# Chunk-selected attention with a capacity-limited expert layer: gating the last head pair from its exponents, and the second expert product in rounds of four 32-column tiles

## Chip, cores and metric

The kernel runs on one core of one Trainium2 chip, in one launch. The metric is the device time of that launch in microseconds (us), as the median of several runs. The engines are PE (matrix multiplication, with PEld for its weight loads), DVE (vector), ACT (scalar, activation functions), POOL (general purpose; it also starts the indirect transfers) and SP (starts most other transfers).

## The reference, cut to what matters

```python
# attention: 4 batches, 8 heads, 768 tokens, 64 wide; keys in chunks of 32
ub = sum over d of max(q * k_min(chunk), q * k_max(chunk))      # causal chunks only
sel = the 6 chunks with the highest ub of each query
scores = where(sel & causal, q @ k.T / 8, -1e9)
attn = softmax(scores);  out = attn @ v
x = out.transpose(0, 2, 1, 3).reshape(3072, 512)                # a row per token
# experts: 8, capacity 80 tokens each
logits = x @ w_gate;  e = argmax(logits);  gate_w = softmax(logits)[e]
for e in range(8):
    tok = the 80 tokens of expert e with the highest gate_w
    h = relu(x[tok] @ w1[e])                                    # 512 -> 1024
    out[tok] = gate_w[tok] * (h @ w2[e])                        # 1024 -> 512
# every other row of the output is zero
```

## The kernel before, in words

**Attention, 16 head pairs.** The loop `for i in range(NP)` (NP is 16) takes two heads of one batch at a time; four pairs make a batch. For each pair PE computes upper bounds (`bounds`, L473), DVE turns them into a table of chunks that are not selected (`bounds_out`, L480 to L492), and PE turns that table over (`unselT`, L498). `scores` then runs six steps, each a product of keys and queries (L510) plus a mask product (L525) into one of two accumulators SC, and ACT takes the exponents into the tile EXB (L530). POOL cuts the causal diagonal out of each exponent tile (L540) and adds the tiles up into ES (L549). `values` multiplies the exponents by V (L560) into OB, and ACT copies the result to oT (L564). The values are not yet divided by the sum of their exponents.

**A pair is finished in the next pair's iteration.** `sums` multiplies oT by the gate weights (L569), which gives the pair's share of the logits, and ES by ones (L583), which gives the sums of the exponents. `sums_out` turns both over on DVE (L574 to L577) and `scale_lg` divides (L614). `rows` transposes oT to token rows (L604), `scale_rows` divides these into the tile xp (DVE L624), and SP stores xp in `x_rows` in DRAM (L626). There is one xp tile: the next write to it waits until the store before has landed.

**Gate and capacity, per batch.** After a batch's fourth pair DVE adds the logits, takes the maximum and the argmax, and ACT the exponent (`gate_in`, `gate_exp`, `gate`: L633 to L647); gt6 holds the winning probability of each token. The 80 best tokens of each expert come from counting, for each token, how many of its expert's tokens are better: `rank_row` spreads gt6 along a row (PE L670, ACT L672), `rank_pred` makes a second row a hair smaller (ACT L675), `rank_cmp` and `rank_diag` compare (DVE), `rank_count` adds the comparisons on PE (L727), `rank_slot` and `rank_hot` turn the counts to slots (DVE L732 to L741), `table` collects slots on PE (L750) and `merge` puts them into the running list of 80 a expert (DVE L746 to L770). The running list is itself kept sorted (`sort_rows`, `sort_rank`, `sort_apply`). For the first three batches this work is spread over the next batch's iterations; the last batch's stands alone behind the loop, with forms of its own (`last_cmp` L712 to L715, `last_diag` L703) and with dummy products `keep_warm` (L814) on PE.

**The last pair.** In iteration 15 the values follow the scores. Behind the loop `sums_last` (L595) adds the exponents from their tiles and then runs `sums_lg` (L569) on oT; so the last batch's gate begins with the last pair's values.

**Experts.** `merge` ends with `idx`, 80 row numbers for each expert. POOL starts a `gather` of these rows from `x_rows` for each expert (L958). `turn` transposes a gathered tile (PE L967, ACT L970), `up` is the product with w1 (PE L978: 32 products of 80 columns) with ACT (L985) and DVE (L987) taking the positive part into hT, and `down` the product with w2: eight accumulated products with hT as the stationary side, 80 columns wide, and 512 columns of w2 moving (L1009). The last expert's is cut into two halves (L994). DVE multiplies by the gate weight gT (L1013, L997), and POOL scatters the 80 rows to the output (L1015). The order on PE is turn(e+1), up(e), down(e-1).

**Order and waits.** All instructions are written in one order by hand; each engine runs its own in that order. The helper `op` derives the waits from named resources that an operation reads and writes. Weights are loaded by POOL (`wload`, L411 and L414): w2 of expert 6 and w1 of expert 7 at the end of iteration 14, w2 of expert 7 into the first part of EXB behind the loop.

## Time and profile before

| what | value |
|---|---|
| median of 3 runs (lowest to highest) | 299.59 us (299.08 to 306.82) |
| the profiled execution | 297.99 us |
| its span, first to last instruction | 296.2 us |
| mean granted PE clock | 0.975 |
| PE busy | 277.8 us (94%) |
| DVE busy | 208.8 us (70%) |
| POOL busy | 233.8 us (79%) |
| ACT busy | 145.0 us (49%) |
| start of the last pair's scores on PE | 231.13 us |
| end of the last pair's values on PE | 245.25 us |
| gt6 of the last batch ready | 250.05 us |
| first gather on POOL | 260.22 us |
| first turn on PE | 262.90 us |
| last product on PE | 290.65 us |

The span is 1.8 us shorter than the execution it belongs to, and that execution is 1.6 us below the median. Times in the text are microseconds from the start of the span. In a list of instructions in order of time a row gives start, duration, engine, line, operation, output and inputs, and in brackets the idle time ahead of it with what ended it; an "x8" means that eight neighbours of one kind are merged. In the chain of waits a row is one stretch of the path that ended last: start, length, and the engine and line that it was spent on.

### The profile page before, as it was taken

To read this page: it belongs to the slowest core of one execution; us is meant where nothing else is said; L and a number is where in the kernel's file an instruction comes from. 1 tells how busy PE (TensorE), PEld (TensorE's weight loads), DVE (VectorE), ACT (ScalarE), POOL (GpSimd) and SP (SyncE) were. 2 spreads that over 40 slices of the span, in tenths; PEclk is the share of its full clock that TensorE was granted. 3 is DMA by queue.
4 is the path that set the end of the run, shared out by engine and by line. 5 is a ranking of instruction groups with operands and counts; after the bars stand their busy time and mean duration, and the time that the engine had idled before them with its cause. 6 is when DMAs were issued, how large, how long until landed. Compare 5 with 4: busy or idle time off the path is not lost.

```text
span 296.2 us, 8268 instructions
## 1 busy us (share of the span) xinstructions
PE 277.8 (94%) x3400; PEld 171.9 (58%) x3402; DVE 208.8 (70%) x561; ACT 145.0 (49%) x197; POOL 233.8 (79%) x299
## 2 busy tenths in 40 slices
PE   7679999999999999999999999999999999579992
PEld 7245565655656565656565657565646566247662
DVE  3867282746797989659889898898897886803332
ACT  2155646565657555545764546566654541512210
POOL 5049999989898999989899999898999993055332
PEclk9779999999999999999999999999999999879999
DMA  9998999998999999999999999899438299511212
GB/s 150 172 156 135 294 190 138 291 229 154 165 159 197 183 164 186 182 187 169 165 186 177 168 174 214 133 192 361 169 69 158 21 175 191 99 41 47 61 45 66
DMA packets 155141, 47.52 MB, mean 160 GB/s; under 512 B 139128, under 2 KB 147444, under 8 KB 155104
## 3 DMA queue, kind: packets, MB, share of 16 engines
q1 hardware_dynamic: 138528, 27.95, 47.9%
q0 software_dynamic: 13440, 18.67, 38.7%
q10 hardware_dynamic: 3136, 0.39, 0.9%
q8 instruction: 26, 0.43, 0.6%
q14 instruction: 11, 0.09, 0.1%
HBM read 53.10 MB, written 10.75 MB: 216 GB/s over the span
## 4 chain that ended last, share of the span: by engine, by line
PE 67%; POOL 16%; DVE 6%; DMA 6%; issue 2%; ACTq 1%; POOLq 0%; ACT 0%; DVEq 0%
PE SC L510 21%; PE OB L560 18%; POOL ES L549 12%; PE SC L525 4%; PE OB L1009 4%; DMA x_rows<-xp 4%; PE SC L978 4%; PE M L583 4%; PE OB L604 3%; POOL EXB L540 3%; PE M L473 2%; PE M L569 2%; PE MB L498 2%; DMA kn<-in_k_dram 1%; DMA qn<-x_rows,idx 1%
## 5 line engine op out<-in xcount | busy, mean ns | idle before, releaser
L530 ACT ACTIVATE EXB<-SC 128x1024 f32<-128x1024 f32 x96 | 86.2, 916 | 49.2 <-PE SC L525 47.9
L549 POOL TENSOR_TENSOR ES<-ES,EXB 128x256 f32<-128x256 f32 (+1 forms) x108 | 105.7, 991 | 4.9
L510 PE MATMUL SC<-qT,kT 64*128 64x512 f32 (+3 forms) x512 | 99.5, 479 | 1.0 <-ACT EXB L530 1.0
L560 PE MATMUL OB<-EXB,vn 128*64 128x256 f32 (+2 forms) x704 | 72.3, 360 | 0.4 <-POOL EXB L540 0.4
L560 PEld LDWEIGHTS OB<-EXB,vn 128*64 128x64 f32 x704 | 47.0, 137 | 23.6 <-issue 9.0
L510 PEld LDWEIGHTS SC<-qT,kT 64*128 64x128 f32 x512 | 42.6, 191 | 25.0 <-issue 15.1
L549 POOL TENSOR_TENSOR ES<-EXB 128x768 f32<-128x768 f32 (+1 forms) x32 | 49.9, 1558 | 2.7
L525 PE MATMUL SC<-unsT,ind 64*128 64x128 bf16 (+5 forms) x256 | 38.3, 294 | 0.8 <-ACT unsT L500 0.8
L564 ACT ACTIVATE oT<-OB 128x512 f32<-128x512 f32 (+1 forms) x32 | 15.6, 489 | 44.3 <-PE OB L560 44.3
L540 POOL TENSOR_SCALAR_AFFINE_SELECT EXB<-EXB 128x256 f32<-128x256 f32 x80 | 35.1, 448 | 0.0
L525 PEld LDWEIGHTS SC<-unsT,ind 64*128 64x128 bf16 x256 | 13.0, 96 | 18.3 <-issue 8.0
L574 DVE STREAM_TRANSPOSE M<-M 128x192 f32<-128x192 f32 x16 | 6.3, 394 | 23.1 <-PE M L583 21.2
L441 DVE STREAM_TRANSPOSE qT<-qn 128x768 f32<-128x768 f32 x16 | 15.6, 972 | 9.4 <-PE SC L525 9.4
L624 DVE TENSOR_TENSOR xp<-OB,rden 128x768 bf16<-128x768 f32 x16 | 15.3, 955 | 7.0 <-PE OB L604 6.1
L445 ACT ACTIVATE rq<-qT 128x768 f32<-128x768 f32 x16 | 13.5, 843 | 9.7 <-DVE qT L441 8.9
L451 DVE STREAM_TRANSPOSE kT<-kn 128x768 f32<-128x768 f32 x16 | 15.5, 967 | 3.6 <-DMA kn<-in_k_dram 3.5
L1015 POOL DMA_INDIRECT out_dram<-EXB,idx x7 | 6.5, 931 | 12.8 <-DVE EXB L1013 7.8
L958 POOL DMA_INDIRECT qn<-x_rows,idx x4 | 3.9, 982 | 15.7 <-DVE gT L770 13.2
L455 DVE TENSOR_REDUCE kmm<-kT 128x24 f32<-128x768 f32 x16 | 15.2, 950 | 0.5
L457 POOL TENSOR_TENSOR kmm<-kmx,kmm 128x24 f32<-128x24 f32 x16 | 7.3, 454 | 10.4 <-DVE wg L833 6.8
L456 DVE TENSOR_REDUCE kmx<-kT 128x24 f32<-128x768 f32 x16 | 15.1, 943 | 0.0
L487 DVE MAX8 top<-M 128x8 f32<-128x8 f32 (+4 forms) x160 | 14.6, 166 | 0.6
(163 smaller groups left out, 404.7 us busy)
## 6 DMA issues: line engine op xcount, KB each, us to landing
w1s<-in_moe_w_dram POOLq DMA_DIRECT2D x8, 1024.0 KB, 9.2
w2s<-in_moe_w_dram POOLq DMA_DIRECT2D x7, 1024.0 KB, 10.6
qn<-in_q_dram SPq DMA_DIRECT2D x64, 96.0 KB, 3.3
vn<-in_v_dram SPq DMA_DIRECT2D x32, 192.0 KB, 3.5
out_dram<-w1s SPq DMA_DIRECT2D x4, 1536.0 KB, 9.1
kn<-in_k_dram SPq DMA_DIRECT2D x60, 96.0 KB, 3.2
x_rows<-xp SPq DMA_DIRECT2D x16, 192.0 KB, 4.7
EXB<-in_moe_w_dram POOLq DMA_DIRECT2D x1, 1024.0 KB, 10.8
```

The source lines that it names most:

```text
L441: op("dve", lambda: ve.transpose(qT[j][:], qn[s][:].rearrange("p a b c -> p (a b c)")), r=[f"qn{s}{g}" for g in range(4)], w=[f"qT{j}"])
L451: op("dve", lambda: ve.transpose(kT[j][:], kn[s][:].rearrange("p a b c -> p (a b c)")), r=[f"kn{s}{g}" for g in range(4)], w=[f"kT{j}"])
L455: op("dve", lambda: ve.tensor_reduce(kmm[j][:, 0, 0:NCH], kv, AX, ALU.min), r=[f"kT{j}"], w=[f"kmm{j}"])
L456: op("dve", lambda: ve.tensor_reduce(kmx[:], kv, AX, ALU.max), r=[f"kT{j}"], w=["kmx"])
L510: op("pe", lambda: pe.matmul(o, kT[j][pr, ts(kt)], qT[j][pr, q0:q1], start=True, stop=False), r=[f"kT{j}", f"qT{j}"], w=[f"SC{s}"], inc=False)
L525: op("pe", lambda: pe.matmul(o, ind[pr, ts(kt)], unsT[j][pr, b0 - 128:q1 - 128], start=False, stop=True), r=[f"ind{h}", f"unsT{j}"], w=[f" ...
L530: op("act", lambda: ac.activation(Ex(st, None, 0, W), src, ACTF.Exp, scale=SCALE), r=[f"SC{s}"], w=[f"E{st}"])
L540: op("gp", lambda: gp.affine_select(ad, a, pattern=[[0, 2], [1, 128]], compare_op=ALU.is_ge, fill=0.0, base=0, channel_multiplier=-1), r=[ ...
L549: op("gp", lambda: gp.tensor_tensor(o, in0, in1, ALU.add), r=[f"E{s2}", f"E{first[0]}"] if first else [f"E{s2}"] + kt, w=kt)
L560: op("pe", lambda: pe.matmul(OB[pr, q0:q1], vn[s][:, kt, h, :], ex, start=(n == 0), stop=last), r=[f"vn{s}{h}", "ES0" if st is None else f ...
L564: op("act", lambda: ac.activation(oT[:, q0:q1], OB[:, q0:q1], ACTF.Copy), r=[f"O{bk}"], w=[f"oT{bk}"])
L624: op("dve", lambda: ve.tensor_tensor(xo, xi, rx, ALU.mult), r=["O0", "O1", "rden"], w=["xp"])
```

## The change

1. **Last pair's logits from the exponents.** V of the last pair is loaded a second time, in the layout of keys (`load_vk`, four transfers on SP in iteration 12), turned over on DVE (`vw_turn`) and multiplied by the gate weights on PE (`vw_mm`). The result VW has for each key the head's share of 8 logits, and ones in the columns for the sums. The new `sums_last` multiplies the exponent tiles by VW, and gives logits and sums together. It needs neither oT nor ES: POOL leaves out the additions of the last pair and only cuts the diagonals.
2. **Values behind the gate.** The last pair's `values` move behind `sums_last`; the gate, the row of gt6 and a part of the comparisons are written among them. `rows` and `scale_rows` of the last pair come later, in the middle of the comparisons.
3. **Comparisons without the second row.** `rank_pred` is gone for the last batch: `last_low` (less than) and `last_high` (at most) compare with the one row, which is copied in two halves by ACT and DVE (`last_row`). Each token tile needs a lower part, the diagonal and an upper part. The dummy products stand between the counts (`last_count`).
4. **Work of the batch before.** `rank_hot`, the digits and the columns of batch 2 move ahead of `bounds_out` in iteration 14 (`rank_late`), its `table` and `merge` from iteration 15 to the end of 14; `sort_rows` and `sort_rank` move forward in iteration 15; both halves of `clear_xg` stand in iteration 14.
5. **Second expert product in rounds.** Each expert's 80 columns of hT are padded to 96, three blocks of 32. A round takes four blocks, each as the stationary side of a product of its own on 32 columns of PE, each with its own expert's w2 moving. Four experts make three rounds; six rounds replace eight `down`s. `spread` brings gate weights and row numbers to the 128 rows of each round (PE, DVE). A scatter has 128 rows, and there are six.

```diff
+                def vw_turn():
+                    op("dve", lambda: ve.transpose(kT[0][:], kn[0][:].rearrange("p a b c -> p (a b c)")),
...
+                    op("dve", lambda: ve.memset(VW, 0.0), w=["qT0"])
...
+                def vw_mm():
+                    p = (NP - 1) % NPB
+                    for kt in range(NT):
+                        op("pe", lambda: pe.matmul(MBf[:, kt * 16:kt * 16 + 16], kT[0][:, ts(kt)], wg[:, p, 0:16], start=True, stop=True),
...
+                def sums_last():
+                    pieces = [(0, 0, 0, 0, 512), (0, 3, 0, 512, S), (1, 1, 0, 128, 640), (2, 2, 0, 256, S), (4, 3, 256, 512, S),
+                              (3, 4, 0, 384, S), (1, 4, 384, 640, S), (5, 5, 0, 640, S)]
+                    for n, (kt, st, c0, q0, q1) in enumerate(pieces):
                         for h in range(2):
+                            a = Ex(st, h, c0, q1 - q0).rearrange("p (t c i) -> p t c i", c=4, i=32)
                             for c in range(4):
+                                op("pe", lambda: pe.matmul(M0[c * 32:c * 32 + 32, q0 // 4:q1 // 4], VW[:, h, kt, :], a[:, :, c, :],
...
+                    op("act", lambda: ac.activation(G[:, S:S + 384], SC[1][:, 0:384], ACTF.Copy), r=["SC10"], w=["growA"])
+                    op("dve", lambda: ve.tensor_copy(G[:, S + 384:2 * S], SC[1][:, 512:896]), r=["SC11"], w=["growB"])
...
+                def last_low(jt, e):
+                    n = jt * 128
+                    o, x = Cl(jt, 0, n), G[:, S:S + n]
+                    if e == "dve":
+                        op("dve", lambda: ve.tensor_scalar(o, x, gt6[:, jt:jt + 1], None, ALU.is_lt), r=["gt6"] + gk(0, n), w=[f"L{jt}"])
...
+                def last_high(jt):
+                    n = (jt + 1) * 128
+                    op("dve", lambda: ve.tensor_scalar(Cl(jt, n, S - n), G[:, S + n:2 * S], gt6[:, jt:jt + 1], None, ALU.is_le),
...
+                    if i == NP - 1:
+                        sort_rows(True)
+                        vw_mm()
                     if i:
                         sums(i - 1)
                         scale_lg(i - 1)
...
                     if i:
+                        if i == NP - 1:
+                            sort_rank(0)
                         rows(i - 1)
                         scale_rows(i - 1)
+                        if i == NP - 1:
+                            sort_rank(1)
+                    if i == NP - 2:
+                        rank_late(bb)
...
-                sums_last(NP - 1)
+                sums_last()
+                sort_apply()
                 scale_lg(NP - 1)
-                rows(NP - 1)
-                sort_apply()
                 gate_in(b)
                 gate_exp()
+                values(NP - 1, (0,))
+                values(NP - 1, (1,), (0, 3))
+                gate(b)
+                gate_cols(b)
+                for e in range(4):
...
+                sort_take()
+                gate_digits(b)
+                last_row()
+                values(NP - 1, (1,), (3, 9))
                 wload(E - 1, 1)
...
+                last_high(0)
+                last_low(5, "act")
+                last_low(4, "act")
+                last_low(3, "act")
+                last_diag(0, 1, 2, 3, 4, 5)
+                last_low(1, "dve")
+                last_high(1)
+                rows(NP - 1)
+                keep_warm(4)
                 scale_rows(NP - 1)
...
+                last_high(4)
+                last_high(3)
+                last_low(2, "dve")
+                last_high(2)
                 gate_gcols(b)
...
+                last_count((0, 5, 1, 4, 2, 3), (2, 2, 2, 0, 0, 4))
                 rank_slot(b)
                 rank_hot(b)
+                op("dve", lambda: ve.tensor_copy(dT[:, 2, :], gT[:]), r=["gT", "dT"], w=["dT"])
                 table(b)
                 merge(b)
...
+                ROUNDS = [[(0, 0), (0, 1), (0, 2), (1, 0)], [(1, 1), (1, 2), (2, 0), (2, 1)], [(2, 2), (3, 0), (3, 1), (3, 2)]]
...
+                def down(r):
+                    last = r == 5
+                    groups = [(r // 3 * 4 + e, sb) for e, sb in ROUNDS[r % 3]]
+                    o = OB[:, r % 2 * 512:r % 2 * 512 + Dm]
+                    parts = [(o, f"O{r % 2}", 0, Dm)]
+                    if last:
+                        n = Dm // 2
+                        parts = [(o[:, 0:n], f"O{r % 2}", 0, n), (SC[0][:, 0:n], "SC0", n, Dm)]
+                    for o, k, c0, c1 in parts:
                         for fb in range(FB):
+                            for g, (e, sb) in enumerate(groups):
+                                op("pe", lambda: pe.matmul(o[g * 32:g * 32 + 32, :], hTv(e)[:, fb * HW + sb * 32:fb * HW + sb * 32 + 32],
+                                                           w2v(e)[:, fb, c0:c1], start=(fb == 0), stop=(fb == FB - 1)),
...
                 for e in range(3):
                     gather(e)
-                keep_warm(9)
+                spread()
+                keep_warm(13)
                 turn(0)
...
                     up(e)
-                    down(e - 1)
-                down(E - 1)
+                    if e % 4 > 0 and e != 3:
+                        down(e // 4 * 3 + e % 4 - 1)
+                    elif e == 4:
+                        down(2)
```

## The prediction

> **What bounds the kernel now.** I read the page's slices first (PE 9 of 10 nearly throughout, sparse only near the end), then the chain of waits from the last pair on, then that stretch in order of time, then busy time and clock by window. The change touches only the time from pair 14 on, so I look for what ends last there.
>
> The chain:
> ```profile
> 233.44 0.46 PE M L569 x8
> 233.91 0.67 PE M L583 x16
> ...
> 239.40 11.38 DMA x_rows<-xp
> 250.81 0.96 DVE xp L624
> 252.47 0.46 DVE EXB L712
> ...
> 260.22 2.63 DMA qn<-x_rows,idx
> ...
> 263.74 1.96 PE SC L978 x32
> ...
> 266.58 1.78 PE SC L978 x32
> 268.36 1.73 PE OB L1009 x8
> 270.24 1.15 PE SC L978 x32
> 271.39 1.73 PE OB L1009 x8
> ```
> Up to 239 PE bounds. Then the chain names the store of pair 14's xp: the last pair's write of xp waits for it to land. From 250.81 DVE bounds (gate and capacity), and from 263.74 PE again, 1.15 for an up and 1.73 for a down; the first two ups take longer.
>
> The store alone isn't the limit, as the order of time shows:
> ```profile
> 246.46 0.54 PE L569 MATMUL M<-oT,wg 128*32 128x192 f32 x8
> ...
> 249.86 0.19 DVE L646 RECIPROCAL gt<-lsum 128x6 f32<-128x6 f32 x1
> ...
> 250.81 0.96 DVE L624 TENSOR_TENSOR xp<-OB,rden 128x768 bf16<-128x768 f32 x1 [0.39 <-DMA x_rows<-xp]
> ...
> 251.85 0.84 ACT L675 ACTIVATE G<-G 128x768 f32<-128x768 f32 x1
> ```
> DVE waited only 0.39 for it. Two paths end almost together: the store, and values, logits (to 247.0), gt6 (250.05), its row. Removing one lays the other bare. The clock of the last idle stretch:
> ```profile
> 256.00:258.00 2.00, 0.57 (x15) 0.40 (x15) 1.64 (x6) 0.00 (x0) 0.00 (x0) 0.84 0.11 24
> 258.00:260.00 2.00, 1.78 (x9) 0.85 (x9) 0.76 (x5) 0.00 (x0) 0.00 (x0) 0.50 0.00 0
> ```
> Columns: length, busy PE, PEld, DVE, ACT, POOL with counts, PE clock, DMA share, GB/s. PE is granted half speed there; 264 to 268 has 0.57. So the first two ups cost 1.96 and 1.78 where warm ones take 1.15.
>
> **The change, part 1: pairs 14 and 15.** PE gets table (0.35, L750 in the chain), sort_rows (0.55 for eight, from L780) and vw_mm (12 tiny passes, about 0.15) ahead of pair 14's sums or pair 15's scores; the first two ran later before (236.9, 239.5), one of them behind the scores. Scores end at 240.4 instead of 239.6. vw_turn is a 0.97 transpose (L451's row) and two fills (0.4 together); rank_late took 3.1 us in iteration 10 and 4.7 in 14 (L737 to L662: its casts run 0.6 to 1.2 beside POOL's additions, 0.17 without). It moves ahead of bounds_out: 224.8 + 3.5 + 2.3 gives the chunk table at 230.6, and PE needs it at 230.75. So it is hidden, with nothing to spare: at 4.7, PE stands for 1.1. Behind it on DVE queue merge (1.2 to 1.9), eight fills at 0.39 spacing (L838), sums_out of pair 14 (1.7), the sort (2.65), scale_rows(14) (0.95) and the sort's last part (0.85 to 1.3); this ends at 242.9 to 244.0. The store of pair 14 is thus issued at about 242.3, 2.9 later. load_vk adds four 96 KB transfers to SP's queue in iteration 12, behind the loads of that iteration and ahead of the V load; such loads land in 3.2 and have two iterations: nothing.
>
> **Part 2: the gate.** sums_last is 64 products, 5376 columns over the two heads at a quarter of the list (four column tiles side by side, four cycles a column in f32): 2.24 at 2.4 GHz. The old one's 2816 columns are 1.17 by the same count and took about 1.5 (245.18 to 246.7, L595), so 2.7. POOL's cuts stay ahead of it (last exponent 241.4, cut 0.4). From 240.4 logits are ready at 243.1 instead of 247.0. Then as before: sums_out and scale_lg 1.23, gate_in 0.77, exponent to gt6 0.82: 246.0, or 246.9 if DVE is still at the sort; I take 246.4, 3.65 earlier. PE meanwhile runs 1792 of 2560 value columns (3.3 of 4.69), so the row's transposes (0.87) start about 247.0 and end at 247.9; the copies follow.
>
> From gt6 to the first comparison before: 2.33 (250.05 to 252.38). After, on DVE: argmax 0.2, columns 0.26, four fills about 0.5, sort_take 0.45, digits 0.77 (251.69 to 252.46), half the row about 0.45: 2.63. So 3.35 earlier, at 249.0. The dropped second row (ACT 0.84) gains nothing by itself, since DVE was only done with its digits at 252.46.
>
> From the first comparison to the counts' turn before: 3.97 (252.38 to 256.35). After: 640 columns 0.55, six diagonals 1.57, and 128 to 512 columns at 0.27 to 0.47 (0.2 plus their share of the 0.55 row's rest): 2.1 for six; scale_rows 0.96, now inside; less 0.4 of overlap, plus 0.45 for the last counts: 5.2. ACT's three pairs (about 3.9 from 249.8, L714 and L715 scaled) end just in time. So 2.1 earlier; the extra copy into dT takes 0.17. Row numbers are ready 2.0 earlier, and the gather starts at 258.2. Limits: 3.0 if DVE is free early, nothing gained if a wait enters (a rival below). The last store is issued at about 252.8, lands in 2.7 to 5.6 as such stores did when the load's end was near: by 258.2, no wait or a few tenths.
>
> **Part 3: experts' start.** spread (about 0.4) and 13 dummies of 0.213 end 3.6 after the row numbers; the gathered rows land 0.97 + 2.63 = 3.6 after them. Warm, that costs nothing and saves up to 1.96 + 1.78 - 2 x 1.15 = 1.44. At half clock the dummies take 5.5 and delay turn(0) by 1.9 or more. Ten dummies among the counts favour warm: I take -1.0.
>
> **Part 4: rounds.** Before: seven downs at 1.73, two halves 0.89 and 0.87: 13.87. After: a round has 32 products of 512 columns. The nearest row is the counting product, also bf16 with 32-column tiles:
> ```profile
> 222.29 0.28 PE L727 MATMUL MB<-w2s,ohb 128*32 128x32 bf16 x8
> 222.40 0.60 PE L727 MATMUL MB<-w1s,ohb 128*32 128x64 bf16 x36
> ...
> 222.36 0.64 PE MB L727 x44
> ```
> 4608 columns are 1.92 one after another and 0.48 four at a time; the chain has 0.64 for them. So four run at once, with 0.16 to get into this shape. A round is 32 x 512 / 4 / 2.4 GHz = 1.71. Getting in and out again: 0.16, and 0.1 to 0.2 out (a score product behind a product of another shape took 1.06 in the chain, 0.86 behind its own); 0.28 together. Six rounds: 6 x 1.99 = 11.9, which is -1.95; with free changes of shape -3.6.
>
> The Trainium skill speaks against this (TensorE: Matmul & The Clock Gate, Part 3: Packing small matmuls): weight loads overlap running products only where the row group differs, and here all four tiles use all rows; it gives 2.38 times for three column tiles of 512 columns. Scaled to four (an estimate), a round is 6.83 / 3.17 = 2.15, six are 12.9: -0.95 instead of -1.95. If no load overlapped, 32 loads of 0.097 (L727's) would add 3.1 a round. The row shows loads that do hide, for the same shape, and I go by it.
>
> DVE's and ACT's shares per expert stay (0.49, 0.44), products with the gate weight fall from eight at 0.75 to six. Round 0 uses expert 1's hT right after its up; the second half is needed 0.85 after, and takes 0.5. A scatter of 128 rows instead of 80 (0.91 on POOL) costs between nothing and 0.55 more; only the last one counts: +0.2.
>
> **Sum.** -2.0 (gate) - 1.0 (start) - 1.95 (rounds) + 0.2 = -4.75: span 291.5, execution 293.2 against the profiled 297.99. That one lies 1.6 below the median, so on the median's scale 299.6 - 4.8 = 294.8.
>
> **Rivals.**
> - *All of it pays (chance 0.25).* Changes of shape hidden (-3.6), clock full throughout (-1.44), DVE free early (-2.6): -7.4, 292.2. For it: each limit occurs in some row. Against: three at once, and the 0.16 is in the row.
> - *The store takes the place of the values (0.13).* xp for pair 15 stands ahead of four comparisons on DVE. If pair 14's store, now issued at 242.3, again needs 11.4, it lands at 253.7, where DVE wants it at 251.7: +2.0, gain gone in the gate, 296.8. Against: the 11.4 ended with the weight load of 234.52, which landed 16.1 later, at 250.6; a store issued later should still land near there.
> - *Column tiles don't overlap (0.05), slower.* Place: L1107, weight loads between products of one row group. The other terms give -2.8, so the rounds decide from 13.87 + 2.8 = 16.7 on, 2.78 a round, or 2.45 tiles at a time. With no load hidden (1.71 + 3.1): 28.9 plus 1.7, +14, 309; fully one after another 41, 324. The L727 row speaks against both.
> - *The change does little (0.1):* pair 14's DVE queue is late, PE stands, and dummies at half clock delay turn(0): gate -0.5, start +1.0, rounds -1.95: 298.
>
> **How the numbers follow.** Likeliest case, 0.47: 294.8, its own range 293.0 to 296.5 (gate -1.5 to -2.6, start 0 to -1.4, rounds -1 to -2.6). With the first rival at the lower end and the next at the upper: 291.3 to 297.6; outside lie the slow cases and a bit on each side. 2%, about what a measurement of this kernel can tell from no change, is 6.0: below 293.6 falls the first rival but for a tenth, and three eighths of the likeliest case: 0.40. Above 305.6 is 0.04. The rest, 0.56, is within 2%.
>
> **What would show it.** gt6's row of reciprocals near 246.4; the first comparison near 249; no wait of xp on the store above 0.5; first gather near 258.2; ups of 1.15 from the first on; rounds of 1.71 to 2.0 in the chain, ups behind them 0.1 longer. Wrong: rounds above 2.3, a chain through x_rows, scores of pair 15 ending past 241.5, or a half clock while the last dummies run.

## The result, and the profile after

The changed kernel takes 295.94 us (median of 4 runs, 295.82 to 296.48) where the kernel before takes 299.33 (4 runs, 298.98 to 306.82). The ratio is 0.9894, with a 95% interval of 0.9873 to 0.9914: 1.1% less, which counts as the same at the bound of 2%. The prediction was 294.8 with a range of 291.3 to 297.6. Some executions of every kernel (306.82 here) run some per cent longer and stay out of the ratios, and four of the profiles used below, marked * in the table behind the experiments, are of such executions, which had lost most of that time ahead of the gate. A later set of runs of both kernels gave the ratio 0.996 (0.9919 to 1.0001), so the size of the gain is less certain than the first interval says. The profiled execution took 295.82, its span is 294.1 (296.2 before), its mean granted clock 0.994 (0.975). So the total came out about as foretold. Its parts did not: the gate's gain, the largest term of the sum, never reached the experts.

The chain of waits of the changed kernel, from the last scores on (start, length, where; here and in the chains below most pieces under 0.5 are left out):
```profile
240.06 0.84 PE SC L508 x4
241.68 2.54 PE M L623 x126
248.74 0.47 DVE G L700
...
251.95 0.87 DVE xp L650
252.84 6.75 DMA x_rows<-xp
259.65 0.62 issue
260.50 2.79 DMA qn<-x_rows,idx
263.69 0.45 ACT rq L1077
...
264.91 2.58 DMA kn<-x_rows,idx
267.57 0.44 ACT rq L1077
268.38 1.90 PE OB L1107 x29
270.54 1.15 PE SC L1085 x32
271.68 1.88 PE OB L1107 x32
```
Before, a store of xp stood in this chain for 11.38 us in front of the gate. Now another one stands there, beside the gate's last part: the last store, issued at 252.84, lands 6.75 later, behind the row numbers, and the first gather waits for it. The first round too hangs on a transfer: between 264.91 and 268.38 the chain runs through the landing of a gather, a copy on ACT (L1077) and then 29 of the round's 32 products.

Rows in order of time for the gate (start, duration, engine, line, operation, output and inputs, idle time before and what ended it):
```profile
234.26 1.42 PEld L609 LDWEIGHTS MB<-wg,kT 128*128 128x128 f32 x12
234.33 1.45 PE L609 MATMUL MB<-wg,kT 128*128 128x16 f32 x12
...
246.91 0.19 DVE L672 RECIPROCAL gt<-lsum 128x6 f32<-128x6 f32 x1
...
248.54 0.91 POOL L412 DMA_DIRECT2D EXB<-in_moe_w_dram  x1 [5.07 <-PE SC L697]
...
249.23 0.55 DVE L757 TENSOR_SCALAR ES<-G,gt 128x640 bf16<-128x640 f32 x1
...
253.99 0.52 ACT L753 ACTIVATE ES<-ES 128x384 bf16<-128x384 bf16 x1
...
255.10 0.40 DVE L785 STREAM_TRANSPOSE MB<-MB 128x192 f32<-128x192 f32 x1 [1.02 <-PE MB L764]
...
257.74 0.16 DVE L819 SCALAR_TENSOR_TENSOR idx<-dT 80x8 uint32<-80x8 f32 x1
...
260.50 1.05 POOL L1065 DMA_INDIRECT qn<-x_rows,idx  x1 [11.04 <-DMA x_rows<-xp]
```
The gate's weights (L672) are there 2.95 earlier than before (249.86), the row numbers (L819) 1.35 earlier; but the gather stands at 260.50, where it stood at 260.22. It waits 2.60 behind the row numbers, against 0.97 before.

The clock in the stretch that was half granted before (length, then the busy time of PE, PEld, DVE, ACT and POOL with the number of instructions, then PE clock, DMA share and GB/s):
```profile
256.00:258.00 2.00, 0.60 (x7) 0.38 (x6) 1.56 (x8) 0.00 (x0) 0.00 (x0) 1.00 0.95 179
258.00:260.00 2.00, 1.81 (x31) 1.08 (x33) 0.49 (x3) 0.00 (x0) 0.00 (x0) 1.00 0.07 13
```
It is full here and up to the last product.

Where the 2.2 us of span came from, by the two profiles:

| stretch | before | after | difference |
|---|---|---|---|
| start of the gate's reciprocals | 249.86 | 246.91 | -2.95 |
| from there to row numbers ready | 9.40 | 10.98 | +1.58 |
| row numbers to first gather | 0.97 | 2.60 | +1.63 |
| first gather to ACT's copy of the first turn | 3.03 | 3.19 | +0.16 |
| that copy to the end of the second up | 5.11 | 3.74 | -1.37 |
| end of the second up to the last product's end | 22.29 | 21.10 | -1.19 |
| from there to the end | 5.60 | 5.56 | -0.04 |

### The profile page after: what moved, and what is told of

Read it like the earlier page. It is cut to its first block, busy times and chain, and to the rows that moved or that the text cites. A ratio compares the mean times of both kernels' runs of the same rounds, so it can differ in the third digit from the quotient of the medians.

```text
span 294.1 us, 8681 instructions
## 1 busy us (share of the span) xinstructions
PE 275.3 (94%) x3601; PEld 170.7 (58%) x3603; DVE 208.9 (71%) x576; ACT 144.4 (49%) x198; POOL 225.1 (77%) x292
## 4 chain that ended last, share of the span: by engine, by line
PE 65%; POOL 16%; DMA 7%; DVE 6%; issue 3%; ACT 1%; ACTq 1%; POOLq 0%; DVEq 0%
PE SC L508 21%; PE OB L561 19%; POOL ES L547 12%; PE SC L523 4%; PE M L586 4%; PE OB L630 3%; PE OB L1107 3%; POOL EXB L538 3%; PE M L471 2%; DMA x_rows<-xp 2%; PE M L572 2%; DMA kn<-x_rows,idx 2%; PE MB L496 2%; DMA kn<-in_k_dram 2%; PE SC L1085 1%
## 5 line engine op out<-in xcount | busy, mean ns | idle before, releaser
L547 POOL TENSOR_TENSOR ES<-ES,EXB 128x256 f32<-128x256 f32 (+1 forms) x105 | 101.6, 980 | 4.8
L508 PE MATMUL SC<-qT,kT 64*128 64x512 f32 (+3 forms) x512 | 97.8, 472 | 1.0 <-ACT EXB L528 1.0
L561 PE MATMUL OB<-EXB,vn 128*64 128x256 f32 (+3 forms) x704 | 72.6, 361 | 1.5 <-POOL EXB L538 1.5
L561 PEld LDWEIGHTS OB<-EXB,vn 128*64 128x64 f32 x704 | 46.9, 137 | 24.8 <-issue 9.9
L547 POOL TENSOR_TENSOR ES<-EXB 128x768 f32<-128x768 f32 (+1 forms) x30 | 46.7, 1558 | 2.5
L1113 POOL DMA_INDIRECT out_dram<-EXB,idR x6 | 6.0, 997 | 12.6 <-DVE EXB L1111 7.0
L630 PE MATMUL OB<-ident_f,oT 128*128 128x128 f32 x96 | 13.9, 281 | 0.5 <-ACT oT L567 0.5
```

The source lines that it names most:

```text
L508: op("pe", lambda: pe.matmul(o, kT[j][pr, ts(kt)], qT[j][pr, q0:q1], start=True, stop=False), r=[f"kT{j}", f"qT{j}"], w=[f"SC{s}"], inc=False)
L547: op("gp", lambda: gp.tensor_tensor(o, in0, in1, ALU.add), r=[f"E{s2}", f"E{first[0]}"] if first else [f"E{s2}"] + kt, w=kt)
L561: op("pe", lambda: pe.matmul(OB[pr, q0:q1], vn[s][:, kt, h, :], ex, start=(n == 0), stop=last), r=[f"vn{s}{h}", "ES0" if st is None else f ...
L630: op("pe", lambda: pe.transpose(OB[:, ts(t)], oT[:, ts(t)], ident_f[:]), r=["oT0", "oT1", "ident_f"], w=[f"O{t // 4}"], inc=(t in (3, NT - ...
```

## The experiments

Some texts below call PE TensorE, ACT ScalarE, DVE VectorE and POOL GpSimd. Theory after the result: the gate's gain is given back at the last store of xp, which shares the DMA engines with the load of half of expert 7's w2 (1 MB) that the change delays; the rounds lose part of theirs where ACT's copy of turned rows waits for a gather to land and a relu is queued behind it. The rivals were that the store is slow by itself, that the rounds are slow by their own products, that the clock decides everything, and that one of the two halves of the change carries the result alone.

Whole times could not carry fine verdicts: of the kernel before, the runs that enter one ratio spread over 3.7 to 4.3 us in the sets of the experiments. The readings rest on stretches of the profiles, collected in the table behind the experiments.

### The rounds alone

The kernel before with the second product in rounds, its gate as it was:
```diff
-                    up(e)
-                    down(e - 1)
-                down(E - 1)
+                    up(e)
+                    if e % 4 > 0 and e != 3:
+                        down(e // 4 * 3 + e % 4 - 1)
+                    elif e == 4:
+                        down(2)
```
with the new down, hTv, spread and fills. Before its first runs:

> The kernel before with part 5 of the change alone: rounds of four 32-column tiles, the gate as it was. My theory: the rounds give what the changed kernel shows between the end of its second up and its last product, 21.0 instead of 22.3 us, so about -1.3: 298.0 us; the first two ups stay slow (1.96 and 1.78) unless the dummies keep the clock. Rival A, the gate gives all of the 3.4: 299.3 or more. Rival B, the rounds give all of it: 295.9.

Before its second:

> The kernel before with the rounds alone (the gate stays as before). A second look, since the first one's time came from disturbed executions. Theory: the rounds bring 0.9 to 1.5, less where ScalarE's copy waits for a gather (one of two stalls of 0.7 to 1.0 each may fall otherwise, as the gathers start at other times); the start of the experts is that of the kernel before, and its clock too; time 0.3 to 0.6 percent below the kernel before, 297.7 to 298.6 where that one has 299.3. Rival (the gate's part alone carries the result): no difference, within 0.2 percent.

Measured: 1.0031 of the kernel before (0.995 to 1.0112), then 0.9979 (0.9955 to 1.0003), the second from 20 runs, median 297.6. The rounds are worth 0.6 us with an uncertainty of 0.7. That lies below what the theory gave (0.3 to 0.6 percent, here 0.2), though the interval reaches into it, and it doesn't exclude the rival's zero. The chain of the second profile shows a round without a wait and a stalled one:
```profile
273.45 1.86 PE OB L1025 x32
275.56 0.91 PE SC L1003 x16
...
279.39 2.58 DMA kn<-x_rows,idx
282.05 0.44 ACT rq L995
282.87 1.90 PE OB L1025 x29
```
1.86 for 32 products, as in the changed kernel. Ahead of the later one a gather's landing and ACT's copy stand in the chain here too, so this wait belongs to the rounds and not to the gate.

### The gate alone

The changed kernel with the old down and the old loop (the diff above the other way round).

> The changed kernel with part 5 undone: the old eight second products on the new gate. My theory: row numbers come 1.3 us earlier but the gather doesn't, because it waits for the last store of xp; what is left is the full clock in the first two ups, 1.4, less 0.3 of a later gather: about -1.1, 298.2 us. Rival A, the gate gives all of the 3.4: 295.9. Rival B, the gate gives nothing: 299.3. The two parts, measured alone, should add up to the whole change within 0.5.

> The changed kernel without the rounds: gate and order of the last pairs as changed, second products one expert at a time as before. A second look. Theory (the gain of the gate is given back at the store of xp): the row numbers are ready 1.0 to 1.6 earlier than before after the last scores of pair 15, but the first gather starts 2.3 us or more behind them and within 0.4 of where it did before, and the end moves by less than 0.8 other than through the clock; at a full clock in the first ups up to 1.4 earlier besides. Rival (the gate brings its 2.0 and the rounds nothing): the first gather starts 1.5 or more earlier and the time is 0.6 percent or more below the kernel before.

Measured: 0.9949 (0.9843 to 1.0055), then 297.56 to 305.39 in four runs, too few for an interval. So whether the two halves add up to the whole can't be told from times. The chain of the second:
```profile
252.83 6.68 DMA x_rows<-xp
259.56 0.62 issue
260.40 2.65 DMA qn<-x_rows,idx
...
263.95 1.74 PE SC L1061 x32
266.09 0.45 ACT rq L1053
266.59 1.99 PE SC L1061 x32
268.58 1.73 PE OB L1092 x8
```
The gate is as early as in the changed kernel, the row numbers are ready at 257.91, and the gather starts at 260.40, 0.18 later than before. In the first profile it starts 3.18 behind the row numbers. That is the theory; the rival (a gather 1.5 or more earlier) falls. The first ups took 1.74 and 1.99, in the first profile 2.31 and 2.32, where the changed kernel has 1.15 or little more: the dummies among the counts and ahead of the experts are the same in both, so they don't ensure the clock.

### The last weights earlier

The load can start as soon as the values have used the place it goes to. So the values that read this part come first, with a semaphore event of their own (the argument True), and the load directly behind them:
```diff
-                values(NP - 1, (0,))
-                values(NP - 1, (1,), (0, 3))
+                values(NP - 1, (0,), (0, 2))
+                values(NP - 1, (1,), (0, 2), True)
+                wload(E - 1, 1)
+                values(NP - 1, (0,), (2, 9))
+                values(NP - 1, (1,), (2, 3))
...
-                wload(E - 1, 1)
```

> The changed kernel, with the value products that read the first two exponent tiles put first and signalling at once, and POOL's load of expert 7's w2 behind them, so that it is issued near 246.9 instead of 248.5. My theory: the last store of xp is slow (6.75 us) because it shares the transfer engines with this load; the load then ends 1.6 earlier, the store lands near 258.0 instead of 259.65, and the first gather comes 1.6 earlier: 294.3 us. Rival, the store is slow by itself (768 pieces of 256 bytes), whatever the load does: 295.9 us and a landing still 6 to 7 us after its issue.

> The changed kernel with the early last load of weights alone; a second look. Theory: the store of pair 15 lands in 4.5 to 5.5 instead of 6.75, the first gather starts 0.9 to 1.6 behind the row numbers instead of 2.6, turn(0) is 1.0 to 1.7 earlier against the scores of pair 15; rounds 0 and 3 stand as in the changed kernel (2.4 to 2.9); time 1.0 to 1.7 below the changed kernel at the same clock, 0.983 to 0.987 of the kernel before. Rival (the wait of the first gather isn't on the path, or the landings of the gathers take the gain): first gather nearer by that much, time the same as the changed kernel's 0.989 to 0.990.

Measured: 0.9868 (0.9772 to 0.9965, with only two runs of this kernel in it), then 0.9934 (0.9898 to 0.9969), above what theory and rival gave. Of the second profile:
```profile
254.21 0.91 POOL L412 DMA_DIRECT2D EXB<-in_moe_w_dram  x1 [3.73 <-PE OB L561]
...
266.17 1.06 POOL L1067 DMA_INDIRECT qn<-x_rows,idx  x1 [11.05 <-DVE gR L1060]
```
The load goes out 0.30 behind the start of the reciprocals instead of 1.63, and the gather starts 1.58 and 1.27 behind the row numbers, both between 0.9 and 1.6. The row numbers are where they were (10.98 behind the reciprocals), and the store is issued at the same place (5.94). Only the load moved, and 1.0 to 1.6 of the wait went. The events of landing say how the two belong together:

| kernel | load issued, landed | last store issued, landed | row numbers ready |
|---|---|---|---|
| before | 246.12, 256.89 | 251.80, 257.43 | 259.25 |
| changed | 248.54, 259.09 | 252.84, 259.60 | 257.90 |
| early load, second profile | 254.21, 264.69 | 259.85, 265.27 | 264.89 |
| paced, early load (below) | 249.87, 260.05 | 255.50, 260.74 | 260.55 |

The store lands 0.5 to 0.8 behind the load, in 13 of the 14 profiles of this document (1.64 in the other). Since only the load was moved, how long the store takes depends on when the load ends. That the two share the DMA engines is the theory's reading of this tie. And the rival of a store that is slow by itself falls: the store took 6.75 in the changed kernel and 5.4 and 5.7 here.

But the end doesn't show it. In the first profile the clock halved just behind the row numbers, and the 13 dummies took 4.67. In both the stretch from the first turn to the last product is longer, 26.2 and 26.5 instead of 24.8; both are among the marked profiles, but the one with paced gathers below, which isn't, has 25.6. Why, the next runs show.

### The gathers without the wait on ACT

The wait of ACT's copy comes from a name: a gather lists the turned rows of three experts before as read, so the next copy into them must wait for its landing. First the name was dropped:
```diff
-                        r=XD + ["idx"] + ([f"xT{(e - 3) % 2}"] if e > 2 else []), w=[xgk(e)], dsem=f"d_g{e}")
+                        r=XD + ["idx"], w=[xgk(e)], dsem=f"d_g{e}")
```
alone (two sets of runs) and together with the early load.

> The changed kernel, with the gathers from the fourth on no longer tied to the transposed tiles xT. Tied, the copy into xT on ACT waits for that gather to land, and the positive part of the up just done stands behind it on ACT; rounds 0 and 3 begin right behind that up. My theory: rounds 0 and 3 take 2.85 and 2.54 us instead of 1.9 for this reason; freed, 1.5 us are saved: 294.4 us. Rival, the rounds wait for their weight loads or the change of shape: 295.9 us and rounds 0 and 3 as long as before.

> The changed kernel with one edit: gathers from the fourth expert on do not list the turned rows of an earlier expert as read. A second look, since the first profile had half clock in the rounds. Theory: ScalarE's copy of the turned rows no longer waits for a gather's landing, so the relus follow the ups within 0.2 and rounds 0 and 3 take 1.85 to 2.1 at full clock (2.85 and 2.54 in the changed kernel); from the end of the second up to the last product 19.6 to 20.0 instead of 21.05; the first gather still starts 2.3 to 2.9 behind the row numbers, since the store's landing is untouched. Rival (the relu of round 0 is late for another reason, such as VectorE's share): round 0 stays at 2.5 or more.

> The changed kernel with two edits of the tail together: the products of values that read the first two parts of the exponents are put first, and the last load of weights (the half of expert 7's w2) is issued right behind them; and the gathers from the fourth expert on no longer list the turned rows of an earlier expert as read. Theory (the gate's gain is lost because that load starts late and the last store of xp shares the DMA engines with it; rounds 0 and 3 stand because ScalarE's copy waits for a gather's landing with a relu queued behind it): the load is issued about 1.3 us earlier after gt6, the store lands in 5 to 5.5 instead of 6.75, the first gather starts 0.9 to 1.6 nearer to the row numbers (at most 1.6 behind them instead of 2.6), no gap between an up and the round behind it is over 0.3, rounds 0 and 3 take 1.85 to 2.1 at full clock instead of 2.85 and 2.54; together 1.5 to 2.5 below the changed kernel, so a ratio of 0.982 to 0.985 to the kernel before at an equal clock. Rival A (the store is slow for its own packets, not for the load): lands in 6.5 or more although the load is earlier. Rival B (rounds 0 and 3 are slow by the clock or by the products themselves): they stay at 2.5 or more at full clock. Rival C (the clock's half-speed windows decide): the segments come out as said but the whole time moves by less than 1.

Measured: 0.9985 (0.9892 to 1.0078), 1.015 (1.0023 to 1.0276), and 1.0009 (0.9974 to 1.0044) with the early load: no gain, in one case a loss. The part of the store held. Of the kernel with both edits, in order of time:
```profile
249.53 0.19 DVE L672 RECIPROCAL gt<-lsum 128x6 f32<-128x6 f32 x1
...
249.83 0.91 POOL L412 DMA_DIRECT2D EXB<-in_moe_w_dram  x1 [3.73 <-PE OB L561]
...
260.35 0.16 DVE L819 SCALAR_TENSOR_TENSOR idx<-dT 80x8 uint32<-80x8 f32 x1
...
261.49 1.06 POOL L1067 DMA_INDIRECT qn<-x_rows,idx  x1 [10.75 <-DVE idR L1058]
```
This execution runs 2.6 later from further ahead. The gather follows the row numbers (260.51) after 0.98, as in the kernel before. POOL no longer waits for the store, which was issued at 255.47 and landed at 260.24, 4.77 later (rival A had it at 6.5 or more).

The part of the rounds failed. The chain of the second profile with the single edit:
```profile
264.00 1.33 PE SC L1085 x32
265.36 0.44 ACT qT L1092
265.79 3.20 another core or an unknown queue
269.02 0.45 ACT rq L1077
269.51 2.31 PE SC L1085 x32
```
A stall of 3.20 that neither theory had; 3.22 in the first profile and in the kernel with both edits. ACT waits here only for TensorE's count of finished products. The trace keeps the events by which that count goes up: the last product of the first up started at 265.12, its event came at 268.94, and those of the next two groups, started at 265.27 and 265.84, at 269.00 and 269.06. Three events within 0.12, where the work lay 0.7 apart: the products were not slow, their reports (the events that ACT waits for) were late. Meanwhile POOL issued six gathers one after another, 1.26 to 1.36 from start to start.

So the pace was kept and only the wait taken away. The gather waits for a name of its own that ACT's copy writes and nothing writes again:
```diff
-                        r=XD + ["idx"] + ([f"xT{(e - 3) % 2}"] if e > 2 else []), w=[xgk(e)], dsem=f"d_g{e}")
+                        r=XD + ["idx"] + ([f"pc{e - 3}"] if e > 2 else []), w=[xgk(e)], dsem=f"d_g{e}")
...
-                    op("act", lambda: ac.activation(xTv(e), tp[:, 0:DB * CAP], ACTF.Copy), r=[tk], w=[f"xT{e % 2}"] + k0)
+                    op("act", lambda: ac.activation(xTv(e), tp[:, 0:DB * CAP], ACTF.Copy), r=[tk], w=[f"xT{e % 2}", f"pc{e}"] + k0)
```

> The changed kernel with one edit: the gathers from the fourth on still wait for ScalarE's copy of three experts before (they keep their pace), but the wait is on a name of its own that nothing writes again, so ScalarE's next copy no longer waits for the gather's landing. The earlier edit, which dropped the listed read altogether, let six gathers follow one another at 1.26 each, and behind the first up the completions of TensorE's products came 3.2 late. Theory (the copy's wait for the landing stalls rounds 0 and 3; the 3.2 belongs to the unpaced gathers): no gap of 3 behind the first up; the first relu of each up starts within 0.2 of its half up; rounds 0 and 3 at full clock in 1.85 to 2.1 instead of 2.85 and 2.54; end of the second up to the last product 19.4 to 20.1 instead of 21.05; gathers start 2.3 to 2.9 behind the row numbers as in the changed kernel; time 1.0 to 1.6 under the changed kernel at the same clock, so 0.984 to 0.987 of the kernel before. Rival A (the 3.2 comes with the dropped wait itself, whatever the pace): the gap of 3 is there again and the time is 1 percent or more above the changed kernel's. Rival B (rounds 0 and 3 are bound elsewhere): they stay above 2.4.

And this with the early load:

> The changed kernel with the early last load of weights (issued behind the products of values that read its place, 1.3 to 1.6 earlier against the gate's exponents) and the paced gathers that ScalarE's copies don't wait for. Theory (both losses are undone): the first gather starts 0.9 to 1.2 behind the row numbers instead of 2.6, rounds 0 and 3 take 1.85 to 2.1 at full clock, no gap of 3 behind the first up; 2.4 to 3.0 below the changed kernel at the same clock: 0.978 to 0.982 of the kernel before, 293.0 to 294.0 where that one has 299.4. Rival (the clock takes it back): the two segments shorten as said, but a half clock falls on the first ups or the dummies and the time is within 1 of the changed kernel's, 0.986 to 0.990.

Measured: 0.9956 (0.9934 to 0.9978) and 0.9909 (0.9864 to 0.9953), neither as low as its theory had it (0.984 to 0.987, 0.978 to 0.982). The stall of 3 is gone, so rival A falls. The wait on ACT can now be priced in one of its two places. Round 3 of the changed kernel, and of the kernel with paced gathers and early load:
```profile
279.40 0.40 PE L1107 MATMUL OB<-w2s,qT 128*32 128x512 bf16 x3
280.04 1.90 PE L1107 MATMUL OB<-w2s,qT 128*32 128x512 bf16 x29 [0.24 <-ACT qT L1092]
...
281.45 2.10 PE L1109 MATMUL OB<-w2s,qT 128*32 128x512 bf16 x32
```
In the changed kernel three products run, then PE waits for ACT's relu, and the round takes 2.54. It takes 2.10 to 2.12 in all five profiles without that wait. Round 0 doesn't come down so far: 2.89 and 2.42 (2.86 by the same rows in the changed kernel), with the report of the up ahead of it 1.2 and 0.7 late. So for round 0 the wait on ACT is read from the chain but its removal doesn't show what it costs.

The stretch from the first turn to the last product is still not shorter, 26.4 and 25.6 against 24.8 (3.41 of the 26.4 at half clock). The reports are late in smaller pieces. Of the second kernel:
```profile
265.17 1.32 PE L1087 MATMUL SC<-rq,w1s 128*128 128x80 bf16 x32 [0.53 <-ACT rq L1079]
265.89 0.96 POOL L1067 DMA_INDIRECT kn<-x_rows,idx  x1 [0.63 <-issue]
...
266.59 0.44 ACT L1094 ACTIVATE qT<-SC 128x320 bf16<-128x320 f32 x1 [1.48 <-PE SC L1087]
```
The relu of the first half starts 1.42 behind the up, and in the changed kernel 0.78, although the up's products run as there. It waits for a report that is 0.64 late by the trace's events. In the whole stretch of this kernel rounds 0 and 3 take 0.4 less each than in the changed one, and three waits among late reports, ahead of the second and the fifth up and within the sixth, cost 0.8, 0.45 and 0.2. Together that is about the 0.7 by which it is longer.

### The changed kernel again

A control without an edit, since the changed kernel had only one profile to show.

> The changed kernel itself, unaltered, as the control that the experiments lacked: more executions beside the kernel before, and a second profile of the tail. In eight profiles of the tail (the kernel before among them) the events by which TensorE reports finished products come 0.5 to 3.6 late at some of the experts' products, mostly while GpSimd issues one gather or scatter right behind another; in the only profile of the changed kernel none is late. Theory (the late events are of the chip and the first profile was spared): this profile has at least one event late by over 0.5, from the first turned rows to the last product 25.2 to 26.2 instead of 24.9, and the ratio to the kernel before comes out at 0.991 to 0.995, so that the variants with the early load (0.991 to 0.993) are level with it or below it. Rival (the changed kernel's own pace avoids them, since ScalarE's copies wait there for the landings): none is late by over 0.3, 24.6 to 25.0 at full clock, and the ratio is 0.987 to 0.991. Of both: scores of pair 15, exponents of the gate, row numbers and the store's landing lie against each other as in the first profile, row numbers 10.8 behind the exponents and the first gather 2.3 to 2.9 behind the row numbers.

Measured: 296.12 (14 runs, 295.23 to 299.10), 0.996 (0.9919 to 1.0001) to a kernel before whose runs in this ratio spread from 295.8 to 300.1. The ratio lies outside what theory and rival gave. The times of the changed kernel repeat (295.94 in the first set), those of the kernel before are lower here. Span and tail repeat the first profile within 0.1, but for the store, which takes 0.3 longer, and with it the first gather:
```profile
252.66 7.05 DMA x_rows<-xp
...
264.93 2.58 DMA kn<-x_rows,idx
267.59 0.44 ACT rq L1077
268.41 1.90 PE OB L1107 x29
```
No report is late here, as in the first profile, and the stretch takes 24.80. The theory that the first profile was only spared falls; the rival's picture (the changed kernel avoids the late reports) holds for two profiles of two, though why its pace avoids them isn't shown. The clock gives one more reading:
```profile
260.00:262.00 2.00, 2.00 (x6) 0.75 (x5) 0.00 (x0) 0.00 (x0) 1.08 (x2) 0.50 0.00 0
```
Here the half clock (258.9 to 262.3 in the clock's record) did come, on the dummies, and cost nothing, because the gathered rows landed only behind them: first turn at 263.36 and 263.33. The late gather is the cover.

The stretches of all profiles. "Late" counts the reports over 0.3 behind their product's end in the tail and gives the longest, of two profiles the larger. Outside the tail none of the 14 profiles has one, and the events of DVE, ACT and POOL are nowhere over 0.3 late.

| kernel | load behind the reciprocals | gather behind row numbers | first turn's copy to last product | of it at half clock | late, longest |
|---|---|---|---|---|---|
| before | -3.73 | 0.97 | 27.40 | 3.41 | 7, 2.49 |
| changed, two profiles | 1.63, 1.64 | 2.60, 2.90 | 24.84, 24.80 | 0, 0 | none |
| rounds alone (*, -) | -3.73, -3.73 | 0.97, 0.97 | 26.23, 27.25 | 0, 3.41 | 10, 1.14 |
| gate alone | 1.63, 1.63 | 3.18, 2.50 | 28.14, 26.66 | 6.74, 3.41 | 7, 0.91 |
| early load (*, *) | 0.30, 0.29 | 1.58, 1.27 | 26.17, 26.53 | 0, 0 | 11, 1.24 |
| name dropped (*, -) | 1.62, 1.63 | 2.88, 2.57 | 29.76, 30.18 | 10.24, 6.83 | 10, 3.60 |
| name dropped, early load | 0.30 | 0.97 | 30.06 | 6.83 | 10, 3.59 |
| paced | 1.62 | 2.82 | 26.39 | 3.41 | 7, 1.19 |
| paced, early load | 0.30 | 1.08 | 25.56 | 0 | 11, 1.25 |

The last one has the earliest end of the products, counted from the reciprocals: 40.67, where the changed kernel has 41.61 and 41.79. As a whole it can't be told from it (0.9909 against 0.9894 and 0.996).

## Why the prediction was right, and where it was not

The total fell into its range, but not because the steps held. By the spans less than half of the foretold 4.75 came (2.2). The medians differ by 3.39, since the profiled execution of before lay below its median; by the later ratio of 0.996 it would be 1.2. That the number agrees is in good part luck. By the prediction's own steps:

- **Scores of the last pair at 240.4.** They ended at 241.6. vw_mm was put at 0.15 by its 192 columns, and took 1.29 in the chain. The rows above suggest what counts: the trace lists twelve loads of 128x128 fp32 weights, 1.42 together, each for 16 columns (two for each of the six products). A mis-sized term, 1.1.
- **Sums at 2.7, gt6 at 246.4.** 2.54, and 247.1 (the end of the L672 row): the 1.1 above, less what the sums and the logits' chain took less. The count behind it (2.24, where the old sums were 1.17 by the same count and took about 1.5) fits here, and its 2.4 GHz is what the old second product gives: 8 x 512 columns in 1.73.
- **The store of pair 14 lands before xp wants it.** Right; the rival in which it takes the place of the values did not come about there.
- **First comparison 249.0, from there to the counts' turn 5.2.** 249.23 and 5.87. DVE stood 1.02 before the turn, waiting for PE's last counts. These wait for ACT's last comparison, which ended at 254.51, and stand behind a pair of dummies that ran until 254.68. ACT's comparisons "end just in time" by the prediction, beginning at 249.8; they began at 250.59, behind a copy of the values, and took the 3.9 foretold. So the row numbers were 1.35 earlier, not 2.0.
- **"The last store ... lands by 258.2, no wait or a few tenths."** This step failed. It landed at 259.6, and the wait, 1.63 longer than before, took the remaining 1.35 and 0.28 more. The step took the length of stores near the end of a load. But the change also moved the load's start: from 3.73 ahead of the reciprocals to 1.63 behind them, 2.4 later in the span. Store and load run side by side in both kernels, and the store lands about 0.5 behind the load in both; before that was 1.8 ahead of the row numbers, now it is 1.7 behind them. The early load moved that start alone by 1.33, and the wait shrank by 1.0 to 1.6. The prediction had this tie in hand: its rival on the store of pair 14 says that the 11.4 ended with a weight load. It wasn't asked of the last store, nor when the load that the change set behind the gate's row would end.
- **Experts' start -1.0.** -1.37 by the two profiles, nearly all of it clock: 1.96 and 1.78 for two ups became 1.15 and 1.25. But the kernel with the same gate and the old products had half clock there in both profiles. The term is right for the profiles compared; that the dummies bring it was not shown.
- **Rounds -1.95.** As profiled -1.19, and 0.8 of the 22.29 before was lost in an up that ran in pieces among late reports (from 276.12 to 278.25, where others take 1.3). Without it the rounds bring 0.4; against the gate alone, whose same stretch is 21.5, they bring 0.4. Their own speed was better than foretold: 1.86 to 1.88 for 32 products against 1.99. The row of the counting products was the right guide here, and the 2.15 worked out from the Trainium skill (TensorE: Matmul & The Clock Gate, Part 3: Packing small matmuls) too slow: four tiles over all rows ran at 6.83 / 1.87 = 3.7 times one after another. What was missed is the wait on ACT: round 0 took 2.85, from 267.43 to 270.28, and round 3 2.54, from 279.40 to 281.94. That gives back up to 1.6, of which the experiments show 0.4 (round 3). The prediction had the relus' durations, not what stands ahead of them in ACT's queue.
- **Last scatter +0.2.** The end behind the last product is 5.56, against 5.60: nothing.

In the sum: gate +0.42 up to the first turn's copy instead of -2.0, start -1.37 instead of -1.0, rounds and late reports -1.19 instead of -1.95, last scatter -0.04 instead of +0.2. That is -2.2 in the spans. One sum of the prediction is off and changes nothing here: its rival without overlapping loads gives +14, which from 299.6 is 314 and not 309.

Settled is where the gate's gain went: to the last store, which lands with the delayed load. That the rounds lose to ACT's queue is shown for round 3 and read from the chain for round 0. That undoing both does not make a visibly faster kernel is shown, with the late reports as the reason that the profiles give. What holds the reports back stays open. The pace of POOL's gathers matters (the 3.2 went with it), but it can't be all, since the changed kernel issues a scatter and a gather 0.3 apart as well, and has none late. Nor is it excluded that the recording has a part in it: a transfer's landing is told by 16 events, and of the some 3,400 the twelve profiles with late reports lack 35 to 72, the two without 7 and 10.

## What to carry to other kernels

When a chain is shortened, list the transfers that start from it or are issued behind it, and ask which of them will now run together with the one that the end waits for: here a load whose start moved by 5.4 us against the gate, and with its end the landing of a store, took all of a gain of 1.35. When a wait is taken from a cheap engine, see what its landing was pacing. And a term of clock, read off one profile of each kernel, should be read in a second one before it is called the change's.

## What the runs showed of the hardware that was not expected

- Reports of finished products can come late, by up to 3.6 us, while the products themselves run on time. It happened in 12 of 14 profiles, the kernel before among them, only on PE and only in the stretch in which POOL issues gathers and scatters. The three profiles with the dropped name agree in the resulting stall within 0.02 (3.22, 3.20, 3.22), so it goes with the program rather than with chance.
- Six fp32 products of 16 columns, each with weights of its own, which the trace lists as twelve, take 1.29 in the chain: 0.107 for one of the twelve, about what its weight load takes (1.42 for the twelve).
- A store of 192 KB that SP issues while a 1 MB load of POOL is under way lands 0.5 to 0.8 behind the load in 13 of 14 profiles: 6.7 to 7.4 after its issue where the load began 4.3 us ahead of it, 4.8 to 5.7 where it began 5.6 ahead.
